# Dealt units of d_ff, an earlier request of q and k, and a moved load of w_out in a fused attention and swish layer

## The chip, the cores and the metric

The kernel runs on one core of one Trainium2 chip. The metric is the device time of one execution in microseconds (us), as the median of several runs. Five engines with a stream of instructions each work side by side and meet only at semaphores: TensorE (PE in the profile, its weight loads in a row of their own, PEld), VectorE (DVE), ScalarE (ACT), GpSimd (POOL) and SyncE (SP). DMAs are issued by SP, ACT and POOL; the bytes are moved by 16 DMA engines which all of these queues share. DMAs that SP issues lie in the queue q1 of the profile, those that POOL issues in q0.

## What is computed

Two layers in a row. The first is attention with a sliding window and sinks over 4 batches, 8 heads, 768 positions and 64 dimensions a head: a position sees the first 4 keys and the last 128. The second is a gated layer without attention:

```
scores = q @ k.T / 8, -1e9 where key >= 4 and not 0 <= query - key < 128
x      = softmax(scores) @ v          # laid out as (3072 tokens, 512)
h      = x @ w_in                     # w_in (512, 2048)
out    = (h * sigmoid(beta * h)) @ w_out   # w_out (2048, 512), beta (2048)
```

Inputs and output are float32; on the chip the operands of the matmuls are bfloat16. The order in which the 2048 hidden columns are taken is free, as long as w_in, beta and the rows of w_out are taken alike.

## The kernel before

**Units and tiles.** Attention is cut into 32 units: `place(n)` gives the batch, the pair of heads and the half of the sequence (384 positions) of unit n. Four units make one tile T of 384 tokens, and there are 8 tiles. For each tile the hidden layer runs in 16 blocks m of 128 hidden columns. `hidden` does four matmuls of 384 columns per block (one for each 128 rows of w_in), and a tanh on ACT follows. `gate` multiplies on DVE. `project` adds up 16 matmuls of 512 columns for each of the three groups of 128 tokens (t) in a tile. So a tile can't be started in `hidden` until its four units are through attention, and no `project` can run before the gate of its block and its two-row load of w_out.

**Loads.** `load_w_in(m, 4)` brings all 512 rows of w_in for four blocks (512 columns, 1 MB of float32) and casts to bfloat16 on the way. There are four of these, at m = 0, 4, 8 and 12. `load_w_out(m, 2)` brings the 128 rows of block m and the 128 of block m+1 (512 KB, cast on the way, 256 KB in SBUF); there are eight. Both are issued by POOL. q and k of units 0 to 11 come as float32 by `load_qk` on SP (192 KB each), are cast by `cast` (for units from 4 on all on POOL), turned by TensorE in `transpose_in`, and copied back. Units from 12 on are landed as bfloat16 by POOL (`land_qk`, `land_v`, two DMAs for each of q, k and v) and turned by a DMA on SP (`turn`). `load_v(1, c)` brings v of units 4 to 7 by three DMAs on POOL.

**The order.** The program isn't emitted in the order in which it is written. `Prog` collects operations with their reads, writes and an assumed duration, and `Prog.round` places them by a list schedule: at each step the operation that can start first on its engine, and among equals the one written first. DMAs are given landing times by `landings`, in which the queues share the 16 engines by weights (3.0 for w_in and w_out, 1.0 for q and k, 0.4 for v), and an issue waits while 8 earlier DMAs of its queue are open (`RING`). The order so found is fixed in each engine's stream. In the run every engine takes its stream strictly in that order, so an operation whose input is late holds all behind it. An edit of one load can thus move instructions of all engines.

**The start, as far as the change touches it.** The order of writing is: constants, the load of beta, q and k of units 0 to 3, v of these, attention of units 0 to 3 (`transpose_first`, `first_scores`, `attend`), the four loads of w_in between them, and at n == 2 of that loop the loads of units 4 to 7. There q and k of these units wait for the write of `("w_in", 0, 4)`, which is the second load of w_in, since that load is what writes blocks 4 to 7. After them come the masks, the sinks of v, three loads of v and the first load of w_out. The hidden blocks of tile 0 and the attention of units 4 to 7 follow, mixed by the schedule; the casts of units 4 to 7 are written at steps -1, 0, 1 and 2, the other loads of w_out at steps 0 and 2. q and k of unit n (8 to 11) wait for `("w_out", 2 * n - 12)`, the loads of rows 4, 6, 8 and 10; v of the next tile waits for rows 6 and 8.

beta is laid out with block m in column m of `beta_half`: the load brings 16 rows of 128, one float32 transpose on TensorE turns them, and a DVE instruction halves them.

Of the kernel before, what the change touches and what calls it, by code (L numbers as in the profile page):

```python
# [5 lines left out]
F32 = mybir.dt.float32  # L6
AF = mybir.ActivationFunctionType
ALU = mybir.AluOpType

B, H, S, D = 4, 8, 768, 64  # L10
NSINK, WINDOW = 4, 128
DM, DF, NOUT = 512, 2048, 512
NTOK = B * S
NPAIR = B * (H // 2)
SCALE = 1.0 / (D ** 0.5)
# [3 lines left out]
TT = 384  # L19
NT = NTOK // TT  # L20
NU = 4 * NT
NM = DF // 128
# [33 lines left out]
AGENDA = {}  # L56
for n in range(4, 8):
    for step, at in (("in", n - 4), ("sink", 16), ("a", 16), ("b", 16), ("av", 17), ("out", 18)):
        AGENDA.setdefault(at if step == "in" else at + 1 * (n - 4), []).append((n, step))
for n in range(8, NU):  # L60
    for at, step in STEPS.items():
        AGENDA.setdefault(FIRST[n] + at, []).append((n, step))
# [294 lines left out]
def bass_streamingllm_window__then__act_swish_beta_kernel(  # L357
# [21 lines left out]
    def sb(name, shape, dtype):  # L379
        ctx.append(nc.sbuf_tensor(name, list(shape), dtype))  # L380
        return ctx[-1].__enter__()
# [4 lines left out]

    xT = sb("xT", (128, 4, NTOK), BF16)
    w_in16 = sb("w_in16", (128, 4, DF), BF16)
    w_out16 = sb("w_out16", (128, NM, NOUT), BF16)
    beta_stage = sb("beta_stage", (16, 128), F32)  # L390
    beta_half = sb("beta_half", (128, NM), F32)
    ones = sb("ones", (128, 128), BF16)
    zeros = sb("zeros", (128, 384), BF16)
# [2 lines left out]
    ident32 = sb("ident32", (32, 32), F32)  # L396
# [27 lines left out]
    P = Prog()  # L424
    op = P.op

    def pe(n):
        return {"busy": 2.5 + n / 2.4, "lag": 260.0}
# [142 lines left out]
           w=[("qkT", pb, half)], dma=f"t{pb}{half}", busy=1300.0, lag=1300.0)  # L571

    w_in_src = moe_w_in.rearrange("(c p) f -> p c f", p=128)
    w_out_src = moe_w_out.rearrange("(m p) n -> p m n", p=128)

    def load_w_in(m, ms, after=()):
        here = slice(m * 128, (m + ms) * 128)
# [2 lines left out]
           dma=f"wi{m}", late=0.0 if m else 800.0, **transfer(DM * ms * 128 * 4, 385, 740.0, 3.0))  # L580

    def load_w_out(m, ms, after=()):
        op("gp", lambda e: e.dma_start(w_out16[:, m:m + ms, :], w_out_src[:, m:m + ms, :]), after=after,
           w=[("w_out", mm) for mm in range(m, m + ms)],
           dma=f"wo{m}", **transfer(ms * 128 * NOUT * 4, 416, 740.0, 3.0))

# [224 lines left out]
    def hidden_matmul(i, c):  # L811
        T, m = i // NM, i % NM
        bank, name = hidden_bank(i)
        op("pe", lambda e: e.matmul(  # L814
            bank, w_in16[:, c, m * 128:(m + 1) * 128], xT[:, c, T * TT:(T + 1) * TT],
            start=(c == 0), stop=(c == 3)),
           r=[("w_in", c, m), ("xT", T, c)], w=[name], **pe(TT))

# [22 lines left out]
    def project(T, t, m, bank, name, eng="act", cols=slice(0, NOUT), queue="sp"):  # L841
# [19 lines left out]


    constants()
    op("act", lambda e: e.dma_start(beta_stage[:, :], moe_beta.rearrange("(m p) -> m p", p=128)),
       w=["beta_stage"], dma="beta", busy=500.0, lag=100.0)
    for n in range(4):
        for x in range(2):
# [1 line left out]
    for c in range(6):  # L869
# [10 lines left out]

    select(ident32[:, :], ones32[:, :], [[1, 32]], ALU.is_equal, 0.0, 0, -1, ["ones32"], ["ident32"])
    transpose_first(0)
    op("pe", lambda e: nc.tensor.transpose(acc[1][:, 0:16], beta_stage[:, :], ident32[0:16, 0:16]),
       r=["beta_stage", "ident32"], w=["acc1"], **pe(64))
    op("dve", lambda e: e.tensor_scalar(beta_half[:, :], acc[1][:, 0:16], 0.5, None, ALU.mult),
       x=["acc1"], w=["beta"], **dve(100.0))

    def first_scores(n):
# [12 lines left out]
    for n in range(4):  # L901
        if n < 2:
            transpose_first(n + 2)
        if n < 3:
            first_scores(n + 1)
        if n == 2:
            for y in range(4, 8):
                for x in range(2):
                    load_qk(y, x, [("w_in", 0, 4)])
            fill("gp", k_sink[:, :, :], 0.0, ["k_sink"], busy=1800.0, after=[("v", 3, 0, 0)])  # L910
            masks([("v", 3, 0, 0)])
            load_sinks(0, [("v", 3, 0, 0)])
            for c in range(3):
                load_v(1, c, [("v", 3, 0, 0)])
            load_w_out(0, 2, [("v", 3, 0, 0)])
        bank = (acc[1], "acc1") if n < 3 else (h_ps[:, 0, :], "h0")
        attend(n, *bank)
        normalise(n, *bank)
# [122 lines left out]
```

## Time and profile before

| | |
|---|---|
| Time, median of 3 runs | 229.1 us (228.0 to 230.09) |
| Profiled execution | 228.59 us |
| its span | 226.9 us |
| PE busy | 220.0 us, 97% |
| ACT busy | 141.3 us, 62% |
| DVE busy | 132.6 us, 58% |
| POOL busy | 125.7 us, 55% |
| HBM read | 27.34 MB |

The span runs from the first instruction to the last; 1.69 us of the execution's 228.59 lie around it. A matmul's row gives its start and its whole duration, through the array, and the next starts long before it ends. A busy PE can therefore still lose time between the starts of its matmuls. In the rows of the chain of work that ended last, an entry with "DMA" is a wait for a transfer, and one with an engine's name is that engine's own work; the bytes of a casting DMA are counted as they land, two bytes an element.

### The profile page before, as it was taken

The page shows a single profiled execution, that of the slowest core. Times are in us where ns is not written, and L with a number is a line of the kernel's source. Part 1 is how long each engine was busy: PE and PEld are TensorE (multiplying, and loading weights), DVE is VectorE, ACT ScalarE, POOL GpSimd, SP SyncE. Part 2 cuts the span into 40 slices and gives each one's busy share as a digit, 9 for nine tenths or more (in the row PEclk, how much of TensorE's full clock was granted, in tenths as well). Part 3 has the DMA queues.
Part 4 walks back from the last instruction along what each step waited for, and adds up shares of the span by engine and source line. Part 5 has one row for each costly group of instructions (what it writes and reads, how often), then busy time and mean ns, then how long its engine had stood idle before and what let it go on. Part 6 is the DMA issues. An engine that isn't in the chain of part 4 may idle for free.

```text
span 226.9 us, 4463 instructions
## 1 busy us (share of the span) xinstructions
PE 220.0 (97%) x1761; PEld 122.1 (54%) x1761; DVE 132.6 (58%) x264; ACT 141.3 (62%) x224; POOL 125.7 (55%) x191
## 2 busy tenths in 40 slices
PE   7999989999999999999999999999999999999995
PEld 4665545555555555555555555555555555555454
DVE  5466777488975776566565656555656564443200
ACT  1877796197586877566657766666656755555311
POOL 4689992899994979695939396876300000000000
PEclk9999999999999999999999999999999999999999
DMA  6999999999998999999999999998921012110122
GB/s 172 251 172 179 276 194 205 257 228 139 118 138 124 124 117 151 120 167 144 116 113 135 99 138 147 96 165 119 94 80 53 20 57 64 49 46 0 58 83 92
DMA packets 96901, 28.92 MB, mean 127 GB/s; under 512 B 83424, under 2 KB 93936, under 8 KB 96880
## 3 DMA queue, kind: packets, MB, share of 16 engines
q0 software_dynamic: 59232, 10.92, 65.7%
q1 hardware_dynamic: 34304, 16.79, 34.3%
q10 hardware_dynamic: 3344, 0.93, 1.9%
q8 instruction: 14, 0.23, 0.5%
q14 instruction: 7, 0.06, 0.1%
HBM read 27.34 MB, written 6.29 MB: 148 GB/s over the span
## 4 chain that ended last, share of the span: by engine, by line
PE 73%; DMA 15%; POOL 8%; issue 2%; SPq 1%; ACT 0%; POOLq 0%; ACTq 0%
PE acc L843 32%; PE h_ps L814 29%; DMA k_stage<-in_k_dram 8%; DMA w_out<-in_moe_w_out_dram 4%; PE s_ps L727 4%; PE s_ps L770 4%; POOL qk L621 3%; DMA w_in<-in_moe_w_in_dram 2%; POOL land L552 2%; PE h_ps L843 2%; POOL v_aug L561 1%; PE s_ps L759 1%; PE s_ps L670 1%; SPq L522 1%; POOL v_aug L532 0%
## 5 line engine op out<-in xcount | busy, mean ns | idle before, releaser
L822 ACT ACTIVATE th<-h_ps,beta_half 128x384 f32<-128x384 f32 x120 | 69.4, 581 | 59.7 <-PE h_ps L814 59.1
L843 PE MATMUL acc<-w_out,g 128*128 128x512 bf16 x368 | 99.7, 380 | 0.0
L814 PE MATMUL h_ps<-xT,w_in 128*128 128x384 bf16 x480 | 96.2, 326 | 0.0
L835 DVE SCALAR_TENSOR_TENSOR g<-th,h_ps 128x384 bf16<-128x384 f32 x120 | 65.6, 550 | 44.8 <-ACT th L822 44.0
L814 PEld LDWEIGHTS h_ps<-xT,w_in 128*128 128x128 bf16 x480 | 45.6, 98 | 39.8 <-issue 0.8
L843 PEld LDWEIGHTS acc<-w_out,g 128*128 128x128 bf16 x368 | 32.8, 98 | 28.8 <-issue 3.6
L552 POOL DMA_DIRECT2D land<-in_q_dram x40 | 30.2, 760 | 24.0 <-DVE rden L779 24.0
L552 POOL DMA_DIRECT2D land<-in_k_dram x40 | 30.3, 761 | 0.0
L561 POOL DMA_DIRECT2D v_aug<-in_v_dram x40 | 30.2, 760 | 0.0
L735 ACT ACTIVATE E<-s_ps 128x1536 bf16<-128x1536 f32 x20 | 28.8, 1442 | 0.0
L741 DVE TENSOR_TENSOR E<-E,mask 128x1536 bf16<-128x1536 bf16 x20 | 19.2, 958 | 16.4 <-ACT E L735 16.4
L851 ACT ACTIVATE out_sb<-acc 128x512 f32<-128x512 f32 x23 | 13.7, 596 | 7.6 <-PE acc L843 7.4
L770 PEld LDWEIGHTS s_ps<-v_aug,E 128*128 128x128 bf16 x336 | 15.2, 97 | 3.2 <-issue 1.2
L770 PE MATMUL s_ps<-v_aug,E 128*128 128x65 bf16 x336 | 16.8, 193 | 0.0
L707 ACT ACTIVATE E<-s_ps 128x768 bf16<-128x768 f32 x17 | 13.7, 811 | 4.3 <-PE s_ps L700 4.2
L781 DVE TENSOR_TENSOR o_norm<-s_ps,rden 128x384 bf16<-128x384 f32 x28 | 15.6, 556 | 0.8
L714 DVE TENSOR_TENSOR E<-E,mask 128x768 bf16<-128x768 bf16 x16 | 9.0, 572 | 2.0 <-ACT E L707 1.3
L727 PE MATMUL s_ps<-qkT 64*128 64x256 bf16 (+2 forms) x144 | 10.1, 254 | 0.0
L759 PE MATMUL s_ps<-v_sink,E_sink 128*128 128x130 bf16 x48 | 9.3, 219 | 0.0
L621 POOL CAST qk<-k_stage 128x384 bf16<-128x384 f32 x12 | 6.5, 544 | 4.7 <-DMA k_stage<-in_k_dram 4.4
L673 ACT ACTIVATE E_sink<-s_ps 128x384 bf16<-128x384 f32 x16 | 7.8, 490 | 1.5 <-PE s_ps L670 1.5
L727 PEld LDWEIGHTS s_ps<-qkT 64*128 64x128 bf16 x144 | 4.9, 94 | 7.1 <-issue 5.8
(75 smaller groups left out, 155.2 us busy)
## 6 DMA issues: line engine op xcount, KB each, us to landing
out_dram<-out_sb SPq DMA_DIRECT2D x23, 256.0 KB, 2.7
q_stage<-in_q_dram SPq DMA_DIRECT2D x12, 192.0 KB, 7.4
k_stage<-in_k_dram SPq DMA_DIRECT2D x12, 192.0 KB, 7.9
w_in<-in_moe_w_in_dram POOLq DMA_DIRECT2D x4, 512.0 KB, 6.8
w_out<-in_moe_w_out_dram POOLq DMA_DIRECT2D x8, 256.0 KB, 9.6
land<-in_q_dram POOLq DMA_DIRECT2D x40, 48.0 KB, 3.7
land<-in_k_dram POOLq DMA_DIRECT2D x40, 48.0 KB, 4.0
v_aug<-in_v_dram POOLq DMA_DIRECT2D x40, 48.0 KB, 3.4
```

What stands on the lines that cost most here:

```text
L552: op("gp", lambda e, d=d, s=s: e.dma_start(d, s), w=[("land", pb, half, x, hh)], after=after, dma=f"l{pb}{half}{x}{hh}", **transfer(TT * D ...
L561: op("gp", lambda e, d=d, s=s: e.dma_start(d, s), w=[("v", pb, 3 * half + c, hh) for c in range(3)], after=after, dma=f"lv{pb}{half}{hh}", ...
L707: op("act", lambda e: e.activation(both, src[:, :, 0:TT], AF.Exp, bias=0.0, scale=SCALE), x=list(names), w=[("E", n % NE, c)], **act(768))
L727: op("pe", lambda e, at=at, w=w, kb=kb, qb=qb, nq=nq, hh=hh, rows=rows, bank=bank: e.matmul(s_ps[:, 2 * hh + bank, at:at + w], keys_of(pb, ...
L735: op("act", lambda e: e.activation(E[z][:, :, :], src, AF.Exp, bias=0.0, scale=SCALE), x=list(S_NAMES), w=[("E", z, 0), ("E", z, 1)], **ac ...
L741: op("dve", lambda e: e.tensor_tensor(E[z][:, :, :], E[z][:, :, :], m.unsqueeze(1).to_broadcast([128, 2, 768]), ALU.mult), r=[("E", z, 0), ...
L770: last=(x == len(kbs) - 1): e.matmul(av_ps[:, at + hh * D1:at + hh * D1 + D1], E[z][:, hh, col:col + 128], v_aug[:, pb, hh, kb, 0:D1], sta ...
L781: op("dve", lambda e: e.tensor_tensor(o_norm[o][:, :, :, :].rearrange("p m h d -> p (m h) d"), src[:, :, 0:D], rden[z][:, :].unsqueeze(2). ...
L814: op("pe", lambda e: e.matmul(bank, w_in16[:, c, m * 128:(m + 1) * 128], xT[:, c, T * TT:(T + 1) * TT], start=(c == 0), stop=(c == 3)), r= ...
L822: op("act", lambda e: e.activation(th[i % 3][:, :], bank, AF.Tanh, bias=0.0, scale=beta_half[:, m:m + 1]), x=[name], r=["beta"], w=[("th", ...
L835: op("dve", lambda e: e.scalar_tensor_tensor(g[T % 2][:, m, :], th[i % 3][:, :], 1.0, bank, ALU.add, ALU.mult), r=[("th", i % 3)], x=[name ...
L843: op("pe", lambda e: e.matmul(bank[:, 0:width], g[T % 2][:, m, t * 128:(t + 1) * 128], w_out16[:, m, cols], start=(m == 0), stop=(m == NM ...
```

## The change

Four things are done.

- Hidden columns are dealt to blocks in another way. Of each group of 512, block m takes every fourth column, from m % 4. `hidden_matmul` reads its weights with a step of four elements. A load of w_in covers the same four blocks as before.
- With that a partition's rows of w_out for two neighbouring blocks are two neighbouring rows of the matrix: `load_w_out` reads one run of 4 KB for each partition where it read two of 2 KB. beta comes as 4 rows of 512, and four transposes of every fourth column turn it where there was one.
- q and k of units 4 to 7 wait for `("w_in", 0, 0)`, the first load of w_in, where they waited for the second.
- The first load of w_out (two blocks) is written ahead of the three loads of v of units 4 to 7.

The edit of `AGENDA` leaves its values as they were.

```diff
+PER = 4
-        AGENDA.setdefault(at if step == "in" else at + 1 * (n - 4), []).append((n, step))
+        AGENDA.setdefault(at if step == "in" else at + n - 4, []).append((n, step))
-    beta_stage = sb("beta_stage", (16, 128), F32)
+    beta_stage = sb("beta_stage", (NM // PER, 128 * PER), F32)
-    w_out_src = moe_w_out.rearrange("(m p) n -> p m n", p=128)
+    w_out_src = moe_w_out.rearrange("(g p j) n -> p g j n", p=128, j=PER)
 
     def load_w_out(m, ms, after=()):
-        op("gp", lambda e: e.dma_start(w_out16[:, m:m + ms, :], w_out_src[:, m:m + ms, :]), after=after,
+        op("gp", lambda e: e.dma_start(w_out16[:, m:m + ms, :].rearrange("p j n -> p (j n)"),
+                                         w_out_src[:, m // PER, m % PER:m % PER + ms, :].rearrange("p j n -> p (j n)")), after=after,
...
         op("pe", lambda e: e.matmul(
-            bank, w_in16[:, c, m * 128:(m + 1) * 128], xT[:, c, T * TT:(T + 1) * TT],
+            bank, w_in16[:, c, m // PER * 512 + m % PER:m // PER * 512 + 512:PER], xT[:, c, T * TT:(T + 1) * TT],
             start=(c == 0), stop=(c == 3)),
...
-    op("act", lambda e: e.dma_start(beta_stage[:, :], moe_beta.rearrange("(m p) -> m p", p=128)),
+    op("act", lambda e: e.dma_start(beta_stage[:, :], moe_beta.rearrange("(g x) -> g x", x=128 * PER)),
...
-    op("pe", lambda e: nc.tensor.transpose(acc[1][:, 0:16], beta_stage[:, :], ident32[0:16, 0:16]),
-       r=["beta_stage", "ident32"], w=["acc1"], **pe(64))
-    op("dve", lambda e: e.tensor_scalar(beta_half[:, :], acc[1][:, 0:16], 0.5, None, ALU.mult),
+    with P.together("pe"):
+        for j in range(PER):
+            op("pe", lambda e, j=j: nc.tensor.transpose(
+                acc[1][:, j * (NM // PER):(j + 1) * (NM // PER)], beta_stage[:, j:128 * PER:PER],
+                ident32[0:NM // PER, 0:NM // PER]),
+               r=["beta_stage", "ident32"], w=["acc1"], **pe(64))
+    op("dve", lambda e: e.tensor_scalar(beta_half[:, :].rearrange("p (g j) -> p j g", j=PER),
+                                        acc[1][:, 0:NM].rearrange("p (j g) -> p j g", j=PER),
+                                        0.5, None, ALU.mult),
...
                 for x in range(2):
-                    load_qk(y, x, [("w_in", 0, 4)])
+                    load_qk(y, x, [("w_in", 0, 0)])
...
+            load_w_out(0, 2, [("v", 3, 0, 0)])
             for c in range(3):
                 load_v(1, c, [("v", 3, 0, 0)])
-            load_w_out(0, 2, [("v", 3, 0, 0)])
```

## The prediction

> **What bounds the kernel now.** I read the page's shares first, then the chain of work that ended last in order of time, then busy time by stretches. The page says that the chain is mostly PE, but a sixth of it is waiting for transfers:
>
> ```profile
> PE 73%; DMA 15%; POOL 8%; issue 2%; SPq 1%; ACT 0%; POOLq 0%; ACTq 0%
> ```
>
> In order of time (start, duration) the transfers all lie in the first quarter:
>
> ```profile
> 12.45 5.50 DMA w_in<-in_moe_w_in_dram
> ...
> 17.96 0.37 SPq L522
> ...
> 18.37 7.79 DMA k_stage<-in_k_dram
> ...
> 27.81 9.58 DMA w_out<-in_moe_w_out_dram
> ...
> 37.82 7.45 DMA k_stage<-in_k_dram
> ...
> 58.58 0.53 POOL qk L621
> ...
> 59.16 0.34 PE s_ps L634 x3
> ```
>
> The second load of w_in (17.95 us, where its row ends) releases SP's requests for units 4 to 7. The load of w_out blocks 4 and 5 lands at 37.39 and releases those for units 8 to 11. k of unit 8 lands at 45.27, POOL works in a row until the cast of k of unit 11 (58.58), and from 59.16 the chain is PE alone. So two things move the end: when the transfers before 45 us are through, and how much PE loses before 59 us. In front of the 17 us lies the attention of units 0 to 3, which the change doesn't touch. By stretches (start and end, length, then busy PE, PEld, DVE, ACT and POOL, clock, share of DMA, GB/s):
>
> ```profile
> 17.00:26.00 9.00, 8.87 (x58) 5.03 (x55) 6.29 (x13) 7.42 (x15) 9.00 (x20) 1.00 1.15 222
> ...
> 28.90:35.08 6.18, 4.87 (x61) 2.52 (x59) 4.88 (x10) 6.11 (x11) 5.50 (x10) 1.00 1.65 194
> ...
> 60.00:211.00 151.00, 151.00 (x1158) 82.01 (x1157) 89.18 (x170) 98.33 (x152) 77.58 (x103) 1.00 1.00 105
> ```
>
> After 60 us PE is never idle. The one stretch with a real loss is 28.90 to 35.08, between the last hidden block of tile 0 and the first `project`: 6.18 − 4.87 = 1.31 us. As busy time holds the matmuls' drain, the loss is larger. Six transposes take 0.52 us there, one alone 0.22, so starts are 0.06 apart; with the like for the others (18 transposes 1.1, 24 half-height matmuls about 0.9, two sink scores 0.35, 15 of attention 0.75) the 61 need some 3.1 us, and up to 3.1 us are lost:
>
> ```profile
> 28.91 0.52 PE L634 MATMUL s_ps<-ident,qk 128*128 128x128 bf16 x6
> ...
> L634 PE MATMUL s_ps<-ident,qk 128*128 128x128 bf16 x18 | 1.8, 222 | 0.6 <-ACT qkT L641 0.4 <-DVE qkT L641 0.2
> ...
> 35.08 1.04 PE L843 MATMUL acc<-w_out,g 128*128 128x512 bf16 x4
> ```
>
> **The change part by part.**
>
> *Rows of 4 KB.* Between 34 and 37.4 us nothing but w_out moves:
>
> ```profile
> DMA packets 722, 0.70 MB, mean 205 GB/s; under 512 B 42, under 2 KB 722, under 8 KB 722
> ...
> DMA packets 2164, 0.78 MB, mean 194 GB/s; under 512 B 1613, under 2 KB 2161, under 8 KB 2161
> ```
>
> In the first row 1 KB lands per packet; 0.70 MB landed are 1.40 MB read, 412 GB/s. A packet costs 3.4 us × 16 engines / 722 = 75 ns. The second row is 30 to 34 us, with mostly small packets: 4.0 × 16 / 2164 = 30 ns each at most, so a packet's fixed part is at most 30 of the 75 ns. The eight loads land 2 MB in 2048 packets, 128 an engine; with half as many, 64 × 30 ns = 1.9 us is the most that can go, and nothing the least. A load of 512 KB takes 1.3 us at 412 GB/s, already near the best rate of the trace, so I take **0.3 us**, near the low end. [...]
>
> *q and k requested earlier.* SP's stream has only these requests there, so nothing else on it is held or freed. The first load of w_in lands at 8.78 + 5.7 = 14.5, so the eight requests start 3.5 us earlier:
>
> ```profile
> L578 POOL DMA_DIRECT2D w_in<-in_moe_w_in_dram x1: 939/939/939, 8.8 to 8.8; - x1
> ...
> DMA to landing us min/median/max: 5.7/5.7/5.7
> ...
> DMA packets 187, 0.18 MB, mean 125 GB/s; under 512 B 16, under 2 KB 187, under 8 KB 187
> ...
> DMA packets 3462, 1.22 MB, mean 245 GB/s; under 512 B 2167, under 2 KB 3461, under 8 KB 3461
> ## 3 DMA queue, kind: packets, MB, share of 16 engines
> q1 hardware_dynamic: 1381, 0.99, 75.6%
> q0 software_dynamic: 2080, 0.21, 71.0%
> ```
>
> The first DMA row is 17 to 18.4 us, between two loads of w_in: 125 GB/s landed against 205, so 1.4 × (1 − 125/205) = 0.55 us of the engines are unused. Requests that are there by then fill this: **0.5 us**. The second is 25 to 30 us, where q and k move beside the small packets of v: 0.99 + 2 × 0.21 = 1.41 MB read in 5 us, 282 GB/s; at 412 it would take 3.4 us. Up to 1.6 us could be won by mixing q and k with w_in instead; a mix with 768-byte rows won't reach 412 either, and I take **0.4 us**. The other side: w_in shares the engines for longer, and its last load is needed just when it lands:
>
> ```profile
> DMA packets 1766, 1.55 MB, mean 222 GB/s; under 512 B 70, under 2 KB 1766, under 8 KB 1766
> ## 3 DMA queue, kind: packets, MB, share of 16 engines
> q0 software_dynamic: 1007, 1.00, 87.9%
> q1 hardware_dynamic: 759, 0.55, 26.7%
> ...
> PEld acc L814 <- DMA w_in<-in_moe_w_in_dram: 0.5, 1, 0.5
> ```
>
> From 18 to 25 us q1 got 0.55 MB beside w_in, 0.079 MB/us. 3.5 us more of that is 0.27 MB, 0.66 us of the engines; less the filled 0.5, the last load is some 0.2 us later. If all 1.57 MB of the eight loads went first, it would be 3.8 − 0.5 = 3.3 us. The wait of 0.5 us grows by 0.2, not on the chain of transfers.
>
> *w_out ahead of v.* POOL now issues
>
> ```profile
> 22.20 2.68 POOL L542 DMA_DIRECT2D v_aug<-in_v_dram  x3
> 24.85 0.74 POOL L583 DMA_DIRECT2D w_out<-in_moe_w_out_dram  x1
> 25.54 0.56 POOL L621 CAST qk<-q_stage 128x384 bf16<-128x384 f32 x1
> ...
> 32.37 2.11 POOL L583 DMA_DIRECT2D w_out<-in_moe_w_out_dram  x3
> ```
>
> The sum to 25.54 stays, so the casts of unit 4 can't come much earlier than now. The load's 512 KB land ahead of v, and v 1.3 us later. Four `project` matmuls (1.04 us with the drain, 0.9 between starts) can then run before 35 us, in the time PE loses. v's delay moves the first `attend`, whose masks are through just when v lands now; I cost that at nothing, as DMA brings both by the same time as before, and at 1.3 us if PE has nothing to put there.
>
> *Weights with a step.* The loads must stay under the matmuls:
>
> ```profile
> L814 PE MATMUL h_ps<-xT,w_in 128*128 128x384 bf16 x480 | 96.2, 326 | 0.0
> ...
> 17.32 0.65 PE L814 MATMUL acc<-xT,w_in 128*128 128x384 bf16 x3
> ...
> 12.57 0.47 PEld L770 LDWEIGHTS acc<-v_aug,E 128*128 128x128 bf16 x12
> ...
> 3.01 0.17 PEld L883 LDWEIGHTS acc<-ident,beta_stage 16*128 16x128 f32 x1 [0.55 <-DMA beta_stage<-in_moe_beta_dram]
> ```
>
> Three hidden matmuls take 0.65 us and one 0.326: a start every 0.16 us. Twelve weight loads in 0.47 us are at most 0.04 apart. A load may thus take four times as long before it shows. No row has a load with a step; the slowest is the float32 one, 0.17 us. At 0.17 without overlap it would cost 512 × 0.01 = 5 us. I take **0**.
>
> *beta.* Three more small matmuls at 3 us, by the one there
>
> ```profile
> 3.02 0.28 PE L883 MATMUL acc<-ident,beta_stage 16*128 16x16 f32 x1 [0.29 <-DMA beta_stage<-in_moe_beta_dram]
> ...
> 1.89 2.16 DVE L444 MEMSET v_sink<- 128x2080 bf16 x3 [0.36 <-issue]
> ...
> 4.06 0.18 DVE L885 TENSOR_SCALAR beta_half<-acc 128x16 f32<-128x16 f32 x1
> ```
>
> cost 3 × 0.28 = 0.8 us at most. The DVE instruction that reads them stands behind a memset until 4.05, and four would end by 4.15. **0**; uncovered, 0.8 us at the very start.
>
> *Sum.* The transfers before 45 us: 0.3 + 0.5 + 0.4 = 1.2 us earlier, and with them units 8 to 11 and POOL's work. PE must find the same: 0.9 from four `project` matmuls, less 0.2 for w_in, and the rest from the later w_out, which fills PE from 35 us on and now lands earlier. What is late next is again the cast of unit 11. 228.6 − 1.2 = **227.4 us** for an execution like the profiled one, 1.7 us or 0.7% under the median of 229.1. About 1% (2.3 us) is what a measurement of this kernel can tell from no change; the three runs lie 2.1 us apart.
>
> **Rivals.**
>
> *A: both ends give more.* All of the bounds (1.9 + 0.5 + 1.6) would be 4.0, and PE can give at most the 3.1 lost. For it: POOL and PE are both behind those transfers. Against it: 6.11 of 6.18 us of ACT are busy in the lossy stretch, so ACT holds the scores there. With 2.5 to 3.1 won: about 225.8.
>
> *B: hidden anyway.* POOL works from 22.20 to 34.5 without a pause worth a row, and ACT is full; if these two set the pace of units 4 to 7, earlier q and k wait for them and w_out lands when it did. 228.6, give or take 0.5.
>
> *C, slower: w_in starves.* Its mechanism is the one order of each engine. Blocks 8 and 12 stand at fixed places in PE's stream; if the eight loads go first, the last w_in load lands 3.3 us later, and all behind it waits, tanh and exp included. Of the 3.3 us 1.3 are idle now and are taken from later. It decides once the delay is over 1.3 us: 228.6 + 2.0 = 230.6, up to 231.9 if nothing absorbs it. Against it: 0.55 of 2.55 MB is all that q1 got beside w_in.
>
> *D, slower: the step shows.* [...] Under 4 × 0.04 us a load stays hidden; at the float32 row's 0.17 it is 228.6 + 5 = 233.6.
>
> **How the numbers follow.** Forecast 0.40, A 0.25, B 0.17, C 0.13, D 0.05. The range 225.0 to 231.4 goes from a little past A to most of C; D and the tails are left out. Faster by over 1% is under 226.8: A and a third of the forecast, 0.38. Slower by over 1% is over 231.4: D and over half of C, 0.13. The rest is 0.49.
>
> **What would show it.** Packets fall by about 1024, since eight loads land rows of 2 KB. SP's first request after the start is at 14.5. The GB/s at 17 to 18.4 rise to about 200. The last w_in load lands at 25 to 26 (C: past 26.7). w_out lands some 1.2 us earlier, and `project` starts before 33. The hidden rows stay at 0.16 us between starts (D: more). What makes the forecast wrong is an order of the engines' streams that puts casts or transposes where their inputs aren't there yet.

## The result, and the profile after

The changed kernel takes 229.88 us (median of 20 runs, 228.2 to 231.57), the kernel before 228.74 us (20 runs). The ratio is 1.0053 with a 95% interval of 1.0035 to 1.0071: slower by half a per cent, where the forecast had 0.7% faster. The time lies within the range given, but it moved the other way. The profiled execution took 229.1 us, 227.4 of them its span.

On the page, the packets, the shares of the chain of work that ended last, and the rows of the hidden matmuls and of their weight loads (busy, then mean ns of one):

```profile
DMA packets 95853, 28.92 MB, mean 127 GB/s; under 512 B 83412, under 2 KB 91860, under 8 KB 95832
...
PE 81%; DMA 8%; ACT 3%; POOL 3%; DVE 2%; issue 1%; ACTq 1%; POOLq 0%
...
L817 PE MATMUL h_ps<-xT,w_in 128*128 128x384 bf16 x480 | 96.3, 327 | 0.1
...
L817 PEld LDWEIGHTS h_ps<-xT,w_in 128*128 128x128 bf16 x480 | 53.0, 114 | 34.7 <-DVE g L838 1.1
```

The page of before has for the last row:

```profile
L814 PEld LDWEIGHTS h_ps<-xT,w_in 128*128 128x128 bf16 x480 | 45.6, 98 | 39.8 <-issue 0.8
```

There are 1,048 packets fewer (96,901 before). A weight load with a step takes 114 ns instead of 98, and the matmuls over it stay at 327 ns. DMA's share of the chain fell from 15% to 8%, which looks like a success and is none. The chain of the changed kernel in order of time (start, duration) has another transfer in it:

```profile
2.42 6.00 DMA v_stage<-in_v_dram
9.40 0.94 POOL w_in L580
...
16.19 11.51 DMA w_in<-in_moe_w_in_dram
27.74 0.84 PE acc L817 x4
...
46.79 1.31 PE h_ps L817 x8
```

The chain used to pass through the second load of w_in, q and k, w_out, and q and k again. Now it goes from v of units 0 to 3 to the last load of w_in, which lands at 27.7 us where it landed at 25.4, and from there on PE, ACT and DVE in turn are the bound. By stretches (start and end, length, busy PE, PEld, DVE, ACT, POOL, clock, share of DMA, GB/s), the changed kernel first, the kernel before second:

```profile
26.00:35.00 9.00, 8.02 (x69) 4.82 (x67) 7.17 (x13) 7.59 (x13) 7.44 (x16) 1.00 1.52 219
35.00:45.00 10.00, 9.54 (x114) 5.74 (x111) 6.82 (x17) 5.55 (x9) 4.72 (x6) 1.00 1.16 233
45.00:60.00 15.00, 14.91 (x135) 8.67 (x134) 12.49 (x24) 11.06 (x18) 14.99 (x24) 1.00 1.65 185
```

```profile
26.00:35.00 9.00, 7.40 (x79) 4.05 (x77) 7.10 (x13) 7.58 (x14) 8.28 (x15) 1.00 1.55 209
35.00:45.00 10.00, 10.00 (x103) 5.75 (x100) 6.01 (x15) 3.77 (x6) 5.29 (x7) 1.00 1.27 233
45.00:60.00 15.00, 14.34 (x125) 7.96 (x124) 12.65 (x25) 11.51 (x19) 14.66 (x22) 1.00 1.71 165
```

PE is fuller from 26 to 35 us and from 45 to 60, by 0.62 and 0.57 us, and emptier by 0.46 from 35 to 45. The first hidden matmul of tile 1 comes at 46.63 us instead of 44.51. After it the changed kernel needs 227.4 − 46.63 = 180.8 us, the kernel before 226.9 − 44.51 = 182.4. Tile 1 starts 2.1 us later, and 1.6 of that comes back. By then PE has done four matmuls of tile 0's `project` more (32 instead of 28, 0.9 us at 0.216 apart) and six transposes more (0.4), and the wait of 0.47 us for POOL's cast of unit 11 at 59.16 is gone.

**What the early q and k do.** A second profile of the kernel before (`before_again` below) issued its last w_in load at 16.4 us, as the changed kernel did (16.2). The two can be laid side by side. What the queues brought from 14.5 to 25.44 us, and from 14.5 to 27.74 (packets, MB, share of 16 engines; q0 is POOL's queue, almost all w_in, its bytes counted as they land; q1 is q and k). The kernel before:

```profile
q0 software_dynamic: 1775, 1.61, 99.9%
q1 hardware_dynamic: 633, 0.46, 14.2%
...
q0 software_dynamic: 2275, 1.63, 86.2%
q1 hardware_dynamic: 1581, 1.15, 28.9%
```

The changed kernel:

```profile
q0 software_dynamic: 1533, 1.45, 84.5%
q1 hardware_dynamic: 979, 0.72, 26.4%
...
q0 software_dynamic: 2144, 1.62, 79.6%
q1 hardware_dynamic: 1591, 1.16, 33.2%
```

At 27.74 us both have brought the same: 1.63 and 1.62 MB, 1.15 and 1.16 MB. At 25.44 the changed kernel has 0.26 MB more of q and k, and 0.16 MB less in POOL's queue. Nothing was won; w_in, which PE needs first, was put behind q and k.

**What the load of beta does.** ACT's last two requests for v, its table load, and the first scores on PE (start, duration). Before:

```profile
3.44 1.21 ACTq L528 DMA_DIRECT2D v_stage<-in_v_dram  x2
4.68 1.28 ACT L871 ACT_TABLE_LOAD   x1 [4.68 <-issue]
...
6.77 0.34 PE L700 MATMUL s_ps<-qkT 64*128 64x384 bf16 x2 [0.21 <-DVE qkT L659]
```

After:

```profile
3.53 2.02 ACTq L530 DMA_DIRECT2D v_stage<-in_v_dram  x2
5.58 1.28 ACT L874 ACT_TABLE_LOAD   x1 [5.58 <-issue]
...
7.49 0.34 PE L703 MATMUL s_ps<-qkT 64*128 64x384 bf16 x2 [1.60 <-ACT qkT L662]
```

The two requests hold ACT for 2.02 us instead of 1.21. The table load and ACT's copy of `qkT` stand behind them, and PE now waits 1.60 us for that copy, where it waited 0.21, for one of DVE's. What such a delay does to the end is taken up below ("From the hold to the end").

### The profile page after: what moved, and what is told of

Same layout as the page of the kernel before. It is cut to its first block, busy times and chain, and to the rows that moved or that the text cites. A ratio compares the mean times of both kernels' runs of the same rounds, so it can differ in the third digit from the quotient of the medians.

```text
span 227.4 us, 4469 instructions
## 1 busy us (share of the span) xinstructions
PE 220.3 (97%) x1763; PEld 130.4 (57%) x1763; DVE 132.4 (58%) x264; ACT 141.3 (62%) x224; POOL 124.1 (55%) x191
## 4 chain that ended last, share of the span: by engine, by line
PE 81%; DMA 8%; ACT 3%; POOL 3%; DVE 2%; issue 1%; ACTq 1%; POOLq 0%
PE acc L846 35%; PE h_ps L817 31%; DMA w_in<-in_moe_w_in_dram 5%; PE s_ps L773 4%; PE s_ps L730 4%; DMA v_stage<-in_v_dram 3%; PE h_ps L846 2%; ACT E L710 1%; PE s_ps L762 1%; POOL w_in L580 1%; ACT th L825 1%; PE s_ps L673 1%; POOL v_aug L534 1%; DVE g L838 1%; DVE E L717 1%
## 5 line engine op out<-in xcount | busy, mean ns | idle before, releaser
L817 PEld LDWEIGHTS h_ps<-xT,w_in 128*128 128x128 bf16 x480 | 53.0, 114 | 34.7 <-DVE g L838 1.1
L744 DVE TENSOR_TENSOR E<-E,mask 128x1536 bf16<-128x1536 bf16 x20 | 19.2, 958 | 16.2 <-ACT E L738 16.2
```

Of the source, the lines that this page charges most:

```text
L744: op("dve", lambda e: e.tensor_tensor(E[z][:, :, :], E[z][:, :, :], m.unsqueeze(1).to_broadcast([128, 2, 768]), ALU.mult), r=[("E", z, 0), ...
L817: op("pe", lambda e: e.matmul(bank, w_in16[:, c, m // PER * 512 + m % PER:m // PER * 512 + 512:PER], xT[:, c, T * TT:(T + 1) * TT], start= ...
```

## The experiments

Each kernel was timed against the kernel before on the same chip. The first ones were made when the open question was which of two things made the loss: a late start of the whole kernel (the head: beta) or late transfers (the early q and k). Single profiles are a weak instrument here, as executions of one kernel differ by 2 us, so the verdicts come from the ratios and the traces serve for the mechanism. In the table, "held" is the time of ACT's fourth to sixth request for v together (us), "w_in" the landing of its last load, "T1" the first hidden matmul of tile 1, all from the one profiled execution of each, whose own time stands beside them. A ratio is estimated from all runs of the two kernels and needn't be the quotient of their medians.

| kernel | held | w_in | T1 | profiled | median | ratio |
|---|---|---|---|---|---|---|
| before | 1.77 | 25.4 | 44.5 | 228.6 | 228.74 | |
| before_again | 1.87 | 25.5 | 45.3 | 228.7 | 228.54 | 0.999 |
| wo_only | 1.96 | 25.2 | 45.9 | 228.9 | 228.58 | 1.000 |
| d_only | 1.80 | 26.2 | 45.6 | 229.4 | 228.77 | 1.001 |
| wo_dealt | 1.97 | 26.2 | 46.0 | 228.9 | 228.68 | 0.999 |
| beta_turns | 1.83 | 26.3 | 45.6 | 229.7 | 229.03 | 1.000 |
| wo_qk4 | 1.78 | 26.6 | 46.1 | 228.1 | 229.00 | 1.002 |
| qk_only | 1.69 | 27.0 | 46.2 | 228.6 | 229.16 | 1.004 |
| qk_wo | 2.59 | 28.7 | 47.8 | 229.9 | 228.75 | 1.001 |
| all_oldbeta | 3.15 | 29.9 | 48.9 | 231.3 | 229.38 | 1.002 |
| beta_only | 2.26 | 25.0 | 45.2 | 228.6 | 229.68 | 1.005 |
| after_noqk | 2.50 | 25.4 | 45.6 | 228.6 | 229.59 | 1.004 |
| beta_load | 3.08 | 25.5 | 47.1 | 230.5 | 229.87 | 1.006 |
| beta_twice | 3.51 | 25.0 | 48.1 | 232.8 | 232.42 | 1.016 |
| after | 2.58 | 27.7 | 46.6 | 229.1 | 229.88 | 1.005 |
| after_again | 3.08 | 28.1 | 47.5 | 230.0 | 230.13 | 1.007 |

**The two kernels once more.** `before_again` and `after_again` are the kernels unedited.

> The kernel before once more. Theory S (start): ACT's sixth request of v is held until the second load of v has drained (0.65 us in the first profile of before, 0.98 to 2.04 in the five profiles since, four of these with a start that the edit doesn't touch or touches by beta alone), so the first profile of before showed a lucky start: expected here a first hidden matmul between 18.3 and 20 us, not 17.3, and ratio 0.998 to 1.002. Theory H, the one of the runs before (beta's load makes the late start): 17.0 to 17.6 us again.

> The changed kernel once more, on the chip of these runs. H: ratio 1.003 to 1.007 and a first hidden matmul past 18.5 us in this execution too, with ACT's six requests of v near 4 us. R: the same ratio, but a first hidden matmul near 17.3 us in an execution whose mean clock is 1.0.

Measured: 0.9994 [0.9968, 1.0019] and 1.0074 [1.0047, 1.0102]. The loss is there again. The first profile of before had been a lucky one in its start (first hidden matmul at 17.32 us, here 18.95), which alone explains nothing of the end (spans 226.9 and 227.0). Nor is the hold what made it lucky, as `before_again` expected: it is 1.87 us here and 1.77 there.

**beta alone, and all but beta.** `beta_only` is the kernel before with beta in four rows and four transposes of neighbouring columns; `all_oldbeta` is the changed kernel with the old load and transpose, so that beta isn't dealt.

```diff
-    op("act", lambda e: e.dma_start(beta_stage[:, :], moe_beta.rearrange("(m p) -> m p", p=128)),
+    op("act", lambda e: e.dma_start(beta_stage[:, :], moe_beta.rearrange("(g x) -> g x", x=512)),
```

> The kernel before, with beta alone changed: loaded as 4 rows of 512 and turned by four transposes (of neighbouring columns, since the blocks are not dealt). Theory H (head): the load of beta in four rows ahead of v's requests on ACT's queue makes those requests slow (4.14 us for six in the profile after, 3.37 before), ACT's first copy comes 0.9 us late, TensorE idles past 6 us and its clock falls, and the first hidden matmul starts near 19.1 us instead of 17.3: 1 to 2 us slower, ratio 1.004 to 1.009. Theory R (rest): the start of the profile after is one execution's chance and beta costs nothing; the loss lies with the moved loads or the dealt columns: ratio 0.999 to 1.002, first hidden matmul near 17.3 us.

> The changed kernel with beta's load and its one transpose as before; left out is the dealing of beta, so each block's tanh takes the scales of other columns, which costs the same time. H: the 1.2 us forecast for the transfers come through and nothing is lost at the start: ratio 0.993 to 0.998, first hidden matmul near 17.3 us. R: as slow as the changed kernel, ratio 1.003 to 1.007.

Measured: 1.0048 [1.0021, 1.0074] for beta alone, 1.0018 [0.9990, 1.0046] for all the rest. The second lies between the two expectations. The part that I had put at nothing costs at least as much as the others together, though the intervals overlap.

**The two moved loads alone.** `qk_wo` is the kernel before with the early q and k and with w_out ahead of v.

> The kernel before with the two moved loads alone (q and k of units 4 to 7 at the first load of w_in; the first load of w_out ahead of v), columns not dealt, w_out in rows of 2 KB, beta as before. H: most of the gain, ratio 0.994 to 0.999. R, if the moved loads are what loses: 1.003 to 1.007; R, if the dealt columns (4 KB rows, weights with a step) are what loses: 0.994 to 1.000 here and over 1.003 in the changed kernel with the old beta.

Measured: 1.0013 [0.9981, 1.0046]. By its interval this doesn't tell a small loss from none. Its last w_in load lands at 28.7 us, though, 3.3 later than in the kernel before, and PE stands 0.83 us in front of it.

**q and k alone, the changed kernel without them, w_out alone.** In `qk_only` and `after_noqk` one word is edited, in opposite directions; `wo_only` has the other moved load.

```diff
-                    load_qk(y, x, [("w_in", 0, 4)])
+                    load_qk(y, x, [("w_in", 0, 0)])
```

> The kernel before with the one edit that q and k of units 4 to 7 wait for the first load of w_in. Theory C (these loads take their share of the 16 DMA engines from w_in, which is needed first): the last load of w_in lands at 28 to 30 us where it lands at 25.4 in the kernel before, the first hidden matmul of tile 1 comes at 46.5 to 48.5 where it comes at 44.5 to 45.3, k of unit 7 lands no earlier than 31.9; ratio to the kernel before 1.001 to 1.006. Rival (my forecast: the hole between two loads of w_in is filled, w_in 0.2 us later): last load at 25.6, tile 1 no later than 44.5, ratio 0.995 to 0.998.

> The changed kernel with q and k of units 4 to 7 waiting for the second load of w_in again. Theory C (the early q and k make the loss): last load of w_in back at 25 to 26 us, first hidden matmul of tile 1 at 44.3 to 45.5, ratio to the kernel before 0.997 to 1.001, clearly under that of the changed kernel (1.005 to 1.007). Rival (beta in four rows makes the loss, the moves are even): the last load of w_in is back too, but the ratio stays at 1.003 to 1.006.

> The kernel before with the one edit that the first load of w_out stands ahead of the three loads of v. My forecast for this step: four projections run before 35 us in time that TensorE loses, up to 0.9 us, ratio 0.996; last load of w_in at 25.4 as before. Rival (v's delay costs as much as the projections win): v of units 4 to 7 lands 1.3 us later (34.9 where it landed at 33.6), and the ratio is 0.999 to 1.002. If the early q and k are what costs, this kernel must not be slower than 1.001.

Measured: `qk_only` 1.004 [1.001, 1.007], `after_noqk` 1.004 [1.0013, 1.0068], `wo_only` 1.0002 [0.9975, 1.0028]. Issue and time to landing of the last w_in load in `qk_only` and in `after_noqk`:

```profile
L578 POOL DMA_DIRECT2D w_in<-in_moe_w_in_dram x1: 742/742/742, 15.9 to 15.9; - x1
...
DMA to landing us min/median/max: 11.1/11.1/11.1
```

```profile
L580 POOL DMA_DIRECT2D w_in<-in_moe_w_in_dram x1: 740/740/740, 16.0 to 16.0; - x1
...
DMA to landing us min/median/max: 9.4/9.4/9.4
```

So it lands at 27.0 in `qk_only` (25.4 in the kernel before) and at 25.4 in `after_noqk` (27.7 in the changed kernel): the word is worth 1.6 us of landing one way and 2.3 the other, as theory C has it. In `qk_only` the lateness lies below the 28 to 30 expected, and the ratio is the one expected. For `after_noqk` theory C was wrong about the total: w_in is back in its place, and the kernel is still 0.4% slower. So there are two losses, and beta's is the second. In `wo_only` v lands 0.6 us later (34.2), less than the 1.3 expected, and the projections ahead of it win nothing that can be measured: PE stands in front of the first of them until the load of w_out is in.

```profile
31.41 0.38 PE L843 MATMUL acc<-w_out,g 128*128 128x512 bf16 x1 [0.91 <-DMA w_out<-in_moe_w_out_dram]
```

How the early q and k lose their time is shown in part. PE's wait for w_in is in the traces of `after` (0.47 us), `qk_wo` (0.83), `all_oldbeta` (1.65 in two waits) and `after_vsp` below (1.97 in two), while no kernel with late q and k and with beta on ACT has more than 0.12. In `qk_only` and `after_again` there is no such wait: hidden blocks began at 19.3 and 20.6 us there, so PE came to the last ones after the load. Also, the schedule gave these kernels another order. In `qk_only` it differs from that of the kernel before on POOL from 27 us and on ACT and DVE from 35 us. No kernel has the early q and k in the old order, so how much of the loss is the wait and how much the order stays open.

**The dealt columns alone.** `d_only` is the kernel before with the stepped weights and the 4 KB rows.

> The kernel before with the dealt columns alone: weights read with a step of four elements, w_out in rows of 4 KB, beta loaded and turned as before, so beta meets the wrong columns (the dealing of beta is left out; its time is that of the kernel before). My forecast for these two steps: 0 for the weights, 0.3 us less for the rows, ratio 0.998 to 1.000, packets about 1024 fewer. Rival D (the step shows): above 1.005, with the hidden matmuls more than 0.16 us apart. Rival: a gain of more than 0.5 us at the last loads of w_out, which came 1.5 us apart instead of 1.9 in the changed kernel, would give 0.996 or less.

Measured: 1.0008 [0.9988, 1.0028]. Neither a cost of the step nor a gain of the rows shows; ACT, DVE, POOL and SP run in the old order here.

**A part of q and k.** `wo_qk4` puts only the two loads of unit 4 ahead, a quarter of the bytes, beside w_out ahead of v.

```diff
-                    load_qk(y, x, [("w_in", 0, 4)])
+                    load_qk(y, x, [("w_in", 0, 0 if y == 4 else 4)])
```

> The kernel before with w_out ahead of v, and with q and k of unit 4 alone waiting for the first load of w_in; units 5 to 7 wait for the second as before. 0.39 MB go ahead where the eight loads are 1.57 MB. By theory C the delay of w_in goes with the bytes put ahead: a quarter of 2.3 to 4.5 us, last load at 26 to 26.5 us, ratio 0.999 to 1.002. If the hole between two loads of w_in (0.55 us) takes these bytes in, as I forecast for all eight, the last load stays at 25.4 to 25.6 and units 4 to 7 come earlier: 0.996 to 0.998, and this would be the version that beats both kernels.

Measured: 1.0016 [0.9988, 1.0043]; the last w_in load lands 10.6 us after its issue at 16.0.

```profile
L578 POOL DMA_DIRECT2D w_in<-in_moe_w_in_dram x1: 742/742/742, 16.0 to 16.0; - x1
...
DMA to landing us min/median/max: 10.6/10.6/10.6
```

That is 26.6, at the end of what theory C said, so even these 0.39 MB show no gain. But three kernels without early q and k had 26.2 or 26.3 in their executions: the single landing doesn't prove that the delay goes with the bytes.

**Which piece of beta.** `beta_load` has the four-row load and one matmul where the transpose stood; `beta_turns` has the old load and four transposes. In both all other instructions stand in the order of the kernel before. `beta_twice` issues the old load a second time, and there the order did change.

> The kernel before with one edit: beta comes as 4 rows of 512 by ACT, and one float32 matmul of 16 columns on the first 128 of them stands where the transpose stood (turning the rest of beta is left out). All other instructions stand in their old order. Theory L (the load holds ACT: its issue takes 0.56 us instead of 0.43, the six requests of v after it take longer, the table load starts at 5.3 to 6.1 instead of 4.6 to 4.9, and the first scores at 7.2 to 8.0 instead of 6.7): table load past 5.2, ratio 1.002 to 1.006. Theory M (four float32 transposes on TensorE cost it): table load under 5.0, ratio 0.998 to 1.002.

> The kernel before with beta loaded as before and four transposes of its first 4 rows where one of 16 rows stood (so beta is wrong for most columns; turning the other 12 rows is left out). Theory L: as the kernel before, ratio 0.998 to 1.002, table load at 4.6 to 4.9. Theory M: ratio 1.003 to 1.006, with the table load where it was and the first transposes of q later.

> The kernel before with the 16-row load of beta issued twice on ACT, the second time to a tile that nobody reads. Theory L, if what counts is ACT's time before its requests of v: 0.43 us more ahead of them, table load at 5.1 or later, ratio 1.001 to 1.006. If only the shape of the 4-row load counts (its longer rows land ahead of q and v), ratio 0.998 to 1.001 in spite of the later table load.

Measured: `beta_load` 1.006 [1.0031, 1.009], `beta_turns` 1.0001 [0.9969, 1.0032], `beta_twice` 1.0159 [1.0117, 1.0201]. The same rows of ACT and PE as above, of the three in this order:

```profile
3.54 2.52 ACTq L528 DMA_DIRECT2D v_stage<-in_v_dram  x2
6.09 1.28 ACT L871 ACT_TABLE_LOAD   x1 [6.09 <-issue]
...
8.00 0.50 PE L700 MATMUL s_ps<-qkT 64*128 64x384 bf16 x2 [1.16 <-ACT qkT L659]
```

```profile
3.42 1.27 ACTq L528 DMA_DIRECT2D v_stage<-in_v_dram  x2
4.72 1.28 ACT L871 ACT_TABLE_LOAD   x1 [4.72 <-issue]
```

```profile
3.93 2.92 ACTq L529 DMA_DIRECT2D v_stage<-in_v_dram  x2
6.88 1.28 ACT L874 ACT_TABLE_LOAD   x1 [6.88 <-issue]
```

It is the load, not the transposes. Issuing it takes 0.58 us instead of 0.43, but that is the small part: the requests of v behind it are held longer. `beta_twice` shows that the shape of four long rows isn't needed for that: with 0.44 us more on ACT ahead of them the last two requests held ACT for 2.92 us, and the table load came 2.1 us later than in `before_again`. The median rose by 3.6 us, far past the 1.006 expected, but that isn't the load's price alone. The schedule put ACT's second copy of `qkT` (near 8 us in the kernel before) and some later instructions of all engines in other places, and no kernel has the second load without that.

The table's columns go together: with held under 2.0 an execution took 228.1 to 229.7 us, with 2.26 to 2.59 it took 228.6 to 229.9, with over 3 230.0 to 231.3, and in `beta_twice`, with 3.51, 232.8. Two of ten executions with the old load were held long as well (2.59 and 3.15), and all five with the four-row load were (2.26 to 3.08). So a part of the spread between executions of one kernel seems to be this wait, and the four-row load makes the long ones common. That is read from single executions. What sets the length of the hold isn't known: in the two profiles of the kernel before the last request returns within 0.1 us of the landing of the first load of v (4.65 and 4.63 us, 4.74 and 4.67), but in `all_oldbeta` and `after_again` 1.1 and 1.2 us after it, and no run varied that by itself. Nor is it the second load of v, as `before_again` expected: in `before` that one landed at 6.2 us, after the last request had returned at 4.65.

**From the hold to the end.** The traces show one thing that lies between ACT's delay and a late start. A matmul of one form takes about 312 ns at the start of an execution and 219 ns from some point on. From 8 to 11 us, in `before`, `before_again` and `beta_load` (busy, then mean ns of one):

```profile
L450 PE MATMUL acc<-ones 128*128 128x128 bf16 x8 | 0.8, 219 | 0.0
```

```profile
L450 PE MATMUL acc<-ones 128*128 128x128 bf16 x10 | 1.5, 312 | 0.0
```

```profile
L450 PE MATMUL acc<-ones 128*128 128x128 bf16 x8 | 1.2, 311 | 0.0
```

The last slow one of these small matmuls starts at 6.3 us in `before`, 11.4 in `before_again`, 12.7 in `beta_load` and 13.2 in `beta_twice`, and the first hidden matmul follows at 17.3, 19.0, 20.7 and 21.7. In the profile of the changed kernel they are fast from 4.7 us on and slow again from 8 to past 10 us, after PE's wait of 1.60 us; the granted clock is 0.50 from 8 to 11 us. In `before` it is 1.00 from 2 to 8 us, where the small matmuls are slow up to 6.3, so the clock alone doesn't give their pace. Whether PE's wait for ACT decides when the fast pace comes is not shown: the wait wasn't varied by itself, and `before` and `before_again` differ by 5 us in the coming of that pace with the same code.

A late start isn't always paid for. In the nine executions with late q and k that start their hidden blocks between 17.3 and 19.3 us and have all of w_in by 26.3 us, the span is 226.8 to 228.0 us, whatever the start. In `beta_load`, 1.8 us later than `before_again` both there and at tile 1, it is 228.7 (227.0), and in `beta_twice` 231.1. So the four-row load seems to cost where it brings the start past some 19 us, and the profile of `beta_only` (18.84, span 226.8) is one in which it cost nothing.

**ACT relieved.** `before_vsp` and `after_vsp` are the two kernels with the last two requests of v issued by SP; in `after_vsp_betasp` SP also loads beta straight to its 128 x 16 place, in runs of 16 bytes and without transposes.

```diff
-        op("act", lambda e: e.dma_start(v_stage[:, c, 4 * x:4 * x + 4, :], src), w=[("v_stage", x, c)],
+        eng = "sp" if (x, c) in ((1, 1), (1, 2)) else "act"
+        op(eng, lambda e: e.dma_start(v_stage[:, c, 4 * x:4 * x + 4, :], src), w=[("v_stage", x, c)],
```

> The kernel before with the last two of the six requests of v moved from ACT to SP, behind its eight of q and k. S: ACT reaches its table load near 3.5 us and its first copy near 5.4, TensorE has no gap over 1 us between 4 and 9 us, its clock stays at 1.0, the first hidden matmul starts at 16.5 to 17.5 us, ratio 0.990 to 0.997. If the start doesn't matter because transfers set the end: the same start, ratio 0.998 to 1.002.

> The changed kernel with the same two requests moved to SP; beta in four rows on ACT as in the change. S: start as in the kernel before with the moved requests, so beta's price of about 1.1 us (ratio 1.0048 for beta alone) is gone and the loads' gain is seen: 0 to 1.2 us under that kernel, ratio to before 0.986 to 0.996. If beta's price is not the start but its four transposes or its place: 1.1 us over that kernel.

> The same, with beta loaded straight to its place (runs of 16 bytes, no transposes) by SP behind all other early requests, so that ACT's first request is one of v. S: ACT's requests start 0.5 us earlier again; ratio to before 0.985 to 0.994, at or below the run with beta on ACT. If 512 small packets hold up q and k or v: above it.

Measured: 1.0018 [0.9991, 1.0045], 1.0039 [1.0016, 1.0063], 1.0041 [1.0019, 1.0063]. All three gains that were expected are missing. The table load comes at 3.44 and 3.53 us in the first two, and the changed kernel stands 1.0039/1.0018 = 1.0021 over its partner, 0.5 us. That is near the part of q and k, and PE does stand 1.13 and 0.84 us in front of w_in there (the last load lands at 29.9 us), but intervals of this width don't tell 0.5 us from nothing or from twice as much. Taking beta off ACT altogether adds nothing then (1.0041), which fits a load that costs only while ACT is held; its many small packets could have cost something of their own, so it isn't shown. A table load over a microsecond earlier than before doesn't make the kernel faster either: the first exponential then waits for PE's scores and starts at 6.89 us, 0.26 earlier than in the kernel before.

**The change without its costs, twice.** `after_noqk_betasp` is the changed kernel with the late q and k and beta by SP in runs of 16 bytes. `wo_dealt` gets there more plainly, with the old load of beta.

> The changed kernel without its two costly parts: q and k of units 4 to 7 wait for the second load of w_in again, and beta is brought straight to its 128 x 16 place by SP behind the other first loads, without transposes. Theory (the early q and k and the load of beta together make the whole loss): ratio to the kernel before 0.997 to 1.001, last load of w_in at 25 to 26 us, table load by 4.7. If dealt columns or the moved load of w_out cost something that the single runs hid, 1.002 or more.

> The changed kernel without its two costly parts, done in the cleanest way: q and k of units 4 to 7 wait for the second load of w_in, and beta is loaded in 16 rows and turned as before (dealing beta is left out, so it meets the wrong columns; turning it cost nothing by itself). Left are the dealt columns, the 4 KB rows and the load of w_out ahead of v. If the early q and k and the load of beta are the whole loss: table load at 4.6 to 4.9, last load of w_in at 25 to 26 us, ratio 0.997 to 1.001. If something in the two other parts costs only when they are together: 1.003 or more.

Measured: `after_noqk_betasp` 1.0071 [1.004, 1.0103], a clear miss; `wo_dealt` 0.9993 [0.9965, 1.0021]. In the first, the table load was early (4.58 us), but the second load of w_in landed at 21.3 us instead of 18.5, and q and k of units 4 to 7 hang on it: k of unit 4 landed at 27.8 us (25.8 in `after_noqk`), tile 1 began at 48.5. Why that load was late isn't settled. Only this kernel with the late q and k has the small packets of beta, but they had landed at 12.0 us, before that load was requested at 13.1. `wo_dealt` answers the question that was asked: what is left of the change without early q and k and without the four-row load is neither faster nor slower by more than 0.35% (its last w_in load is in at 26.2, a little past the time expected). No kernel was found that beats the one before.

**The parts as a sum.** If every run is taken as a constant plus what its parts cost, least squares over 288 runs of before and of the kernels that isolate parts (without the changed kernel itself, those with loads moved to SP, `beta_twice` and `wo_qk4`) give: the four-row load 0.96 ± 0.14 us, early q and k 0.67 ± 0.16, w_out ahead of v −0.09 ± 0.15, dealt columns with 4 KB rows 0.04 ± 0.15 (standard errors). Their sum is 1.6 us over 228.8. The 32 runs of the changed kernel have a mean of 230.1, 1.3 over it. The two losses can hide each other: in `after_again`, with a late start, PE found w_in already there.

## Why the prediction was wrong

**Rows of 4 KB**, 0.3 us: held as to packets (1,048 fewer, 1,024 forecast), not as to time. With w_out alone under way from 35 to 37.4 us the changed kernel lands

```profile
DMA packets 273, 0.50 MB, mean 208 GB/s; under 512 B 32, under 2 KB 32, under 8 KB 272
```

208 GB/s against 205, and `d_only` moves nothing. The lower end of my bounds was the right one: the trace of the changed kernel has 416 GB/s read with 4 KB rows, that of the kernel before 412 with 2 KB (two bytes read for one landed).

**q and k requested earlier**, 0.5 + 0.4 us won and w_in 0.2 later. This step failed: the edit costs some 0.7 us, and the last load of w_in lands 1.6 us later by itself (`qk_only`) and 2.3 in the changed kernel. Its first half came true: SP starts at 14.99, and between 17 and 18.4 us 198 GB/s land where it was 125.

```profile
14.99 0.37 SPq L524 DMA_DIRECT2D q_stage<-in_q_dram  x1
...
DMA packets 301, 0.28 MB, mean 198 GB/s; under 512 B 13, under 2 KB 301, under 8 KB 301
```

Even the bytes were sized well: I had q1 take 0.27 MB from w_in, and it has 0.26 MB more at 25.44. What was wrong is the time that w_in needs to make up for them. I divided them by the whole rate, 0.66 us, and set the filled hole against that. But q and k keep flowing beside the rest: from 25.44 to 27.74 us POOL's queue brings 1.62 − 1.45 = 0.17 MB, 0.07 MB per us, about a third of the 205 GB/s that w_out has by itself. So the last load is 2.3 us later in this execution, and it lands at 27.0 to 29.9 in the other executions with all eight loads early. Rival C had this: past 26.7, up to 3.3 later, deciding at 1.3. Its time, 230.6, was for a delay of 3.3 us with 1.3 of it absorbed; the runs give the early q and k some 0.7 us by themselves. PE waits only 0.47 us in front of it here, and its weight load 0.65 where it waited 0.5 before, since PE's stream had started later as well (first hidden matmul at 19.08 us, 17.32 in the profile of before). That the wait grew by no more than the 0.2 forecast is luck. The row is:

```profile
27.74 0.84 PE L817 MATMUL acc<-xT,w_in 128*128 128x384 bf16 x4 [0.47 <-DMA w_in<-in_moe_w_in_dram]
```

**Transfers before 45 us 1.2 us earlier**: the sum of these steps, and it came to nothing. The load of w_out that releases q and k of unit 8 is issued 0.6 us later and lands at 37.39 us in both kernels (here its row before, then after):

```profile
L583 POOL DMA_DIRECT2D w_out<-in_moe_w_out_dram x1: 706/706/706, 27.8 to 27.8; - x1
...
DMA to landing us min/median/max: 9.6/9.6/9.6
```

```profile
L585 POOL DMA_DIRECT2D w_out<-in_moe_w_out_dram x1: 568/568/568, 28.4 to 28.4; - x1
...
DMA to landing us min/median/max: 9.0/9.0/9.0
```

w_out's last load lands at 44.3 us (45.1), but k of units 8 to 11 lands at 45.3 to 51.0 as before (45.2 to 50.9). k of units 4 to 7 lands at 23.5, 27.5, 29.6 and 32.4 (26.2, 28.5, 30.1 and 31.9): the lead of 2.7 us is gone by the last one. My rate for mixing (1.6 us at most to be won) supposed engines that were not busy; the windows to 27.74 show that they were. Nor does the trace of before have 412 GB/s for such a mix: from 18 to 25 us w_in beside q and k read 2.55 MB, 364 GB/s. Of the 1.7 us under the median, moreover, only 1.2 were forecast as a gain: 0.5 were the distance of the profiled execution from the median of three, and the 20 runs of the kernel before have 228.74.

**w_out ahead of v**: held in its mechanism, not in its price. `project` starts before 33 and v is 1.1 us later.

```profile
32.11 0.38 PE L846 MATMUL acc<-w_out,g 128*128 128x512 bf16 x1 [0.41 <-DVE g L838]
```

The four `project` matmuls do run before 35 us. That PE is busy 0.62 us more there is not their gain alone, as nine hidden matmuls more fall into that stretch in the later stream. `wo_only` puts the step at zero, with PE idle for 0.91 us in front of the first of the four.

**Weights with a step**, 0: held. Loads of 114 ns stay under matmuls 160 ns apart. Rival D's price rested on 0.17 us for a load, the row of the float32 one, and no run shows that for a load with a step: in the changed kernel one takes 114 ns (110 to 135) against 98. No run here tells what the 16 ns are, and they decide nothing: `d_only` stands at 1.0008.

**beta**, 0: failed, and by the sum above it is the larger loss, 0.96 us, though the errors don't set it apart from the other. I priced the three added transposes and the DVE instruction behind them, and was right about these (`beta_turns`). I didn't price the load. It is the first of seven requests on ACT's queue, and the table load and the copies for the first scores stand behind them. I looked at what waits for beta, and not at what waits behind its request. That the change doesn't touch what lies in front of the 17 us was wrong for that reason.

Rival B has its time, 228.6 give or take 0.5, in `wo_dealt`: the rows and the moved load of w_out by themselves are hidden. Nothing of rival A was seen.

## What to carry to other kernels

Here transfers already filled the DMA engines (the packets of POOL's queue alone took 99.9% of the 16 engines' time from 14.5 to 25.44 us in `before_again`), and an earlier request only reordered them (1.63 and 1.62 MB of that queue were in by 27.74 us). In such a place list the landings in the order in which the engines need them, and ask which one is pushed back, and at what shared rate it finishes. A DMA request takes time of the engine that issues it (0.43 us of ACT for the old load of beta, 0.57 for the four-row one): price the whole row of requests behind it and the work behind these, even for 8 KB. Time a change's parts singly when executions differ by more than the effect; here two losses of under 1 us hid under one number. Where a schedule is worked out anew for each edit, compare the order of the streams too: only a kernel that keeps it isolates the edit.

## What the runs showed of the hardware

ACT was held by the DMAs that it issued. Each of the first four requests for v took 0.42 to 0.56 us, but the sixth took 2.04 in `all_oldbeta` and 2.18 in `beta_twice`; the six together took 3.37 us in the kernel before, 4.63 in `beta_load` and 5.11 in `beta_twice`. With 0.15 us more for one load of 8 KB ahead of them, `beta_load` lost 0.6%. q and k of SP and the casting loads of POOL shared the engines: beside 0.44 MB of q and k POOL's queue brought 0.17 MB from 25.44 to 27.74 us in the changed kernel, a third of the rate that it has alone (0.07 against 0.205 MB/us). A weight load whose columns lie 8 bytes apart takes 114 ns against 98, and `d_only` finds no cost of it under matmuls of 384 columns (1.0008). The same small matmul takes 312 ns early in an execution and 219 ns later, and with the same code the change came at 6 us in one profile and at 11 to 12 in another.
